# Layer 2's first product by seven block products for two of three token chunks

## The chip, the cores and the metric

The kernel runs on one core of one Trainium2 chip. A time is the device time of one execution in microseconds (us); the time of a kernel is the median of its runs. Engines: PE (matrix products), DVE (vector), ACT (scalar, activations), POOL (GpSimd), SP (issues the DMAs). Each works through its own queue in order, and they wait for one another by semaphores.

## The reference

Attention with a window and sink tokens over 1536 tokens, then two feed-forward layers of width 512 to 2048 to 512:

```python
x = attention(q, k, v, n_sink, window)             # 1536 x 512
h = x @ moe_w_in                                   # layer 1
g = (a0 + a1*h + a2*h**2 + a3*h**3) / (1 + |b0|*|h| + |b1|*h**2 + 1e-6)
x = g @ moe_w_out
h = maximum(x @ moe2_w_in, 0)                      # layer 2
out = (h * h) @ moe2_w_out                         # 1536 x 512
```

## The kernel before

**Arithmetic.** The weights come as 64-bit numbers and are turned into fp32 on DVE (three steps, lines 241 to 253) and split on ACT and POOL into a high part in a format that PE takes at full rate and a low rest (`w_fin`, lines 274 and 275). Activations are split in the same way (`gh` and `gl`, lines 685 and 686; `xh` and `xl`). Each product is the sum of three: high by high, high by low, low by high.

**Tiles and steps.** Tokens are in three chunks c of 512, the hidden width in 16 tiles f of 128. A step (L, g, c, f) is one tile of one chunk: the first product `g1` (line 618) is 4 blocks of the width x 3 = 12 matmuls of 128 x 128 by 512 columns into one PSUM bank, tag T (two banks) or U (one); the second product `g2` (line 689) is 4 x 3 = 12 such matmuls, accumulated over the tiles f of a part g in four banks (two tiles `s` of two banks each). `CUTS` cuts the 16 tiles into parts: layer 1 in three, layer 2 in two of 8. After a part `finish` (line 712) reads the four banks, in its first part as a copy (half on DVE, half on ACT), then as an addition on DVE; after the last part of layer 2 it issues the four stores of the chunk on SP.

**Order.** The order of the work is written out by hand: `slot(k)` (line 759) issues, in this order, the split of step k-2 (`act_c`), two weight splits, the end of the activation of step k-1 (`act_b`, which also calls `finish`), `g1` of step k+1, the start of the activation of step k, pending splits of layer 1's results (`split_late`), weight conversion and input checks on DVE up to a due count (`w_until(due(k))`), and `g2` of step k-2. So PE alternates 12 matmuls of a first and 12 of a second product. In layer 2 the activation is a Relu on ACT and a product with the bank on DVE (line 659). K is 96; slots 48 to 95 start the second half of the steps, layer 2. The first `g1` of layer 2 is in slot 47, the last `g2` of layer 1 in slot 49, and its accumulators are read in slot 50 (line 732).

**Weights in layer 2.** 42 of 64 weight tiles are converted before layer 2, the other 22 in its first 22 slots, each followed by a job that reads a weight tile again for a check; then the other checks. `spare` is the list of free weight buffers, taken in order.

**The end.** `verdict()` (line 787) gathers checks of the inputs into a count `fl` on DVE, with one small matmul; it is called after slot 93 and its matmul stands between two slots. After the last slot `values_load` (line 1076) makes every engine load `fl` into a register, and line 1078 branches over a general path that isn't run here.

## Time and profile before

| what | value |
|---|---|
| time, median of 3 runs | 612.98 us (612.82 to 613.57) |
| the profiled execution | 613.21 us |
| its span, first to last instruction | 611.4 us |
| PE busy in the span | 597.7 us, 98% |
| DVE, ACT, POOL busy | 424.8, 342.9, 342.7 us |
| granted clock of PE, mean | 0.996 |

The span is what the trace covers; the execution's own time is 1.81 us longer. A busy PE is not PE at its peak: a matmul's record is longer than the distance to the next one, because matmuls are pipelined, so the price of one is the distance. Rows give the start in the span, the duration, the engine (PEld is the weight load, a q behind the name is the engine's sequencer), the line, the operation, output and input by tile names, and a count of merged instructions.

### The profile page before, as it was taken

Reading aid. Unit: us, or ns where it says so; the run is one execution under the profiler, and the core shown is the slowest. Engines: PE = TensorE matmul, PEld = TensorE weight load, DVE = VectorE, ACT = ScalarE, POOL = GpSimd, SP = SyncE. Lnnn points to the kernel's source line nnn. Section 1 sums busy time; section 2 is a strip of 40 time slices with the busy share of each in tenths; the row PEclk is TensorE's granted clock in tenths of the full one; section 3 lists DMA queues with packets and bytes.
Section 4 is the critical chain, followed back from the end, with each engine's and each line's share of the span. In section 5 each row is a group of like instructions: output and inputs, shape, how many; then the busy total and the mean of one; then the engine's idle time right before and its main releaser. Section 6 shows DMA issues by size and latency. Waiting matters only on the chain.

```text
span 611.4 us, 9769 instructions
## 1 busy us (share of the span) xinstructions
PE 597.7 (98%) x3490; PEld 491.4 (80%) x3490; DVE 424.8 (69%) x855; ACT 342.9 (56%) x727; POOL 342.7 (56%) x316
## 2 busy tenths in 40 slices
PE   8899999999999999999999999999999999999995
PEld 6787788788888878888888888888888888888884
DVE  5989759988988989858768799598583432531411
ACT  5989768788886687877769343333332222222220
POOL 4699878677776676757658475354452222222221
PEclk9999999999999999999999999999999999999998
DMA  7986313333323232111102457377375345600102
GB/s 204 287 219 178 87 38 103 104 103 104 104 70 103 73 101 82 56 36 35 46 24 69 139 176 246 129 228 254 94 247 182 117 161 163 200 8 0 70 0 75
DMA packets 64232, 72.05 MB, mean 118 GB/s; under 512 B 15280, under 2 KB 55216, under 8 KB 64176
## 3 DMA queue, kind: packets, MB, share of 16 engines
q1 hardware_dynamic: 64032, 71.35, 38.2%
q8 instruction: 29, 0.48, 0.3%
q14 instruction: 27, 0.22, 0.1%
q10 hardware_dynamic: 144, 0.00, 0.0%
HBM read 68.20 MB, written 3.15 MB: 117 GB/s over the span
## 4 chain that ended last, share of the span: by engine, by line
PE 71%; DVE 15%; ACT 10%; issue 2%; DMA 1%; DVEq 0%; ACTq 0%
PE s L703 32%; PE T L624 25%; PE U L624 7%; DVE t L678 3%; PE O L470 2%; DVE U L676 2%; ACT U L670 2%; ACT U L671 2%; ACT gh L685 2%; ACT w L274 2%; ACT pe L406 2%; DVE t L674 1%; DVE ns L387 1%; DVE O L241 1%; DVE wx L253 1%
## 5 line engine op out<-in xcount | busy, mean ns | idle before, releaser
L624 PE MATMUL T<-xh,w 128*128 128x512 f32 x640 | 210.9, 391 | 0.4 <-DVE t L653 0.4
L686 POOL TENSOR_TENSOR gl<-g,gh 128x512 fp32r<-128x512 f32 x48 | 62.2, 1296 | 157.8 <-ACT gh L685 157.8
L624 PEld LDWEIGHTS T<-xh,w 128*128 128x128 f32 x640 | 120.1, 188 | 27.6 <-DVE t L653 2.3
L703 PE MATMUL s<-gh,w 128*128 128x512 f32 x384 | 126.1, 389 | 0.0
L624 PE MATMUL T<-xl,w 128*128 128x512 f32 x320 | 124.6, 389 | 0.0
L703 PE MATMUL s<-w,gh 128*128 128x512 f32 x384 | 118.1, 389 | 0.0
L686 POOL TENSOR_TENSOR gl<-t,gh 128x512 fp32r<-128x512 f32 x48 | 62.3, 1297 | 42.8 <-ACT gh L685 42.0
L275 POOL TENSOR_TENSOR w<-wx,w 128x512 fp32r<-128x512 f32 x64 | 82.9, 1296 | 2.9 <-ACT w L274 2.3
L703 PEld LDWEIGHTS s<-w,gh 128*128 128x128 f32 x384 | 72.1, 188 | 15.0
L703 PEld LDWEIGHTS s<-gh,w 128*128 128x128 f32 x384 | 72.0, 188 | 14.9
L645 POOL TENSOR_TENSOR t<-t,ah 128x512 f32<-128x512 f32 x48 | 62.3, 1298 | 34.4 <-ACT t L642 32.5
L685 ACT CAST gh<-g 128x512 fp32r<-128x512 f32 x48 | 29.9, 623 | 82.1 <-PE s L703 74.7
L703 PE MATMUL s<-gl,w 128*128 128x512 f32 x192 | 74.7, 389 | 0.0
L703 PE MATMUL s<-w,gl 128*128 128x512 f32 x192 | 74.7, 389 | 0.0
L624 PEld LDWEIGHTS T<-xl,w 128*128 128x128 f32 x320 | 60.0, 188 | 12.2
L685 ACT CAST gh<-t 128x512 fp32r<-128x512 f32 x48 | 29.8, 622 | 45.5 <-DVE t L678 39.8
L674 DVE SCALAR_TENSOR_TENSOR t<-t,U 128x512 f32<-128x512 f32 x48 | 32.9, 686 | 28.8 <-ACT U L671 28.8
L659 DVE TENSOR_TENSOR g<-r,T 128x512 f32<-128x512 f32 x32 | 21.7, 682 | 42.2 <-ACT r L649 42.2
L649 ACT ACTIVATE r<-T 128x512 f32<-128x512 f32 x32 | 19.2, 600 | 53.2 <-PE T L624 53.1
L703 PEld LDWEIGHTS s<-gl,w 128*128 128x128 f32 x192 | 36.0, 188 | 7.6
L624 PE MATMUL U<-xh,w 128*128 128x512 f32 x128 | 42.1, 390 | 0.0
L406 ACT ACTIVATE pe<-ns,nmax 128x136 f32<-128x136 f32 (+1 forms) x96 | 38.0, 400 | 7.2 <-DVE nmax L387 7.0
(142 smaller groups left out, 1010.5 us busy)
## 6 DMA issues: line engine op xcount, KB each, us to landing
wr<-in_w_in_dram SPq DMA_DIRECT2D x54, 512.0 KB, 3.7
wr<-in_w_out_dram SPq DMA_DIRECT2D x52, 512.0 KB, 3.7
qr<-in_q_dram SPq DMA_DIRECT2D x12, 256.0 KB, 5.4
keys<-in_k_dram SPq DMA_DIRECT2D x12, 256.0 KB, 5.1
vr<-in_v_dram SPq DMA_DIRECT2D x12, 256.0 KB, 5.6
wr<-in_v_dram SPq DMA_DIRECT2D x6, 512.0 KB, 4.7
out_dram<-part SPq DMA_DIRECT2D x12, 256.0 KB, 2.0
vsc<-in_v_dram SPq DMA_DIRECT2D x2, 16.0 KB
```

The lines of the kernel that those rows point to most:

```text
L274: (nc.gpsimd.tensor_copy if conv["tag"] == "U" else nc.scalar.copy)(out=t[:, 0], in_=xf)
L275: nc.gpsimd.tensor_tensor(out=t[:, 1], in0=xf, in1=t[:, 0].bitcast(F32), op=ALU.subtract)
L406: nc.scalar.activation(out=t[:, e, 0:w], in_=ns[e][:, 0:w], func=ACTF.Exp, scale=-1.0, bias=nmax[:, ix:ix + 1], accum_out=rs[:, 2 * pr + e ...
L624: nc.tensor.matmul(h, lhsT=wi[a][:, kk * P:(kk + 1) * P], rhs=(xh, xl)[b][c][:, kk, :], start=(kk == 0 and a + b == 0), stop=(kk == KD - 1 ...
L645: nc.gpsimd.tensor_tensor(out=t, in0=t, in1=ah, op=ALU.mult)
L649: nc.scalar.activation(out=r, in_=h, func=ACTF.Relu)
L659: nc.vector.tensor_tensor(out=g, in0=st.pop(k), in1=h, op=ALU.mult)
L674: nc.vector.scalar_tensor_tensor(out=t, in0=t, scalar=QP, in1=r0, op0=ALU.add, op1=ALU.mult)
L678: nc.vector.scalar_tensor_tensor(out=t3, in0=t3, scalar=fa[:, 0:1], in1=r0, op0=ALU.add, op1=ALU.mult)
L685: nc.scalar.copy(out=gh, in_=g)
L686: nc.gpsimd.tensor_tensor(out=gl, in0=g, in1=gh.bitcast(F32), op=ALU.subtract)
L703: nc.tensor.matmul(acc[L, g, c][m], lhsT=lh, rhs=rh, start=(f == f0 and a + b == 0), stop=(f == f1 and a == 1),)
```

## The change

1. **Seven products for eight.** In layer 2 the first product of the chunks 1 and 2 is computed for pairs of tiles f at a time. With the weights of the pair as 2 x 2 blocks (the two tiles by the two halves of the width) and the tokens as 2 x 2 blocks (the two halves of the width by the two chunks), a group has 7 block products of 6 matmuls each (`product`) in the place of 8. Sums of weight blocks go into the four S products (`weights_sums`, on POOL, then split by ACT and POOL), sums of token blocks into the T products (`tokens_sums`, once, on DVE, right after layer 1's last results; split by `tokens_split` in the turns 3 to 6). DVE adds the block products up (`after`), ACT does Relu and Square (`square`). Chunk 0 keeps the 12 matmuls of a step (`whole`).
2. **Turns.** Layer 2 has its own order: turn n is issued in slot 47 + n. `hs` lists which first products a turn does, `gs` which second product, `ms` and `ss` the turns in which the weight sums and their splits are issued. In the first part the turns 0 to 3 do the four whole steps of chunk 0, turn 4 product 1 of group 0, turn 5 none, turn 6 product 6, the turns 7 to 12 the pairs of `ORDER`; second products stand in the turns 3 to 6, 9, 10 and 13 to 18. In the later parts each turn has 12 matmuls of first products, but for one without, and the second products run six turns behind; the turns 48 to 54 have second products only.
3. **Four parts.** `CUTS` cuts layer 2 in four parts of 4 tiles. The last part of the last chunk accumulates in four single banks (T, T, U and half of an `s`). The order of the weight tiles follows; the 22 late conversions have turns of their own (`CONV`), one check is due in each turn, and at most 11 weight tiles of layer 2 are held (`LIVE`).
4. **The flag.** The first half of `verdict` stands after turn 49, its matmul after turn 52, and the load of the flag after turn 53, before the last turn.

```diff
-CUTS = ((0, 4, 9, 16), (0, 8, 16))
+CUTS = ((0, 4, 9, 16), (0, 4, 8, 12, 16))
 AHEAD = 10
+LIVE = 11
+GAP = 2
+TURN = 12
+CONV = (1, 9, 10, 12, 13, 15, 16, 17, 18, 19, 20, 22, 23, 27, 28, 29, 30, 31, 32, 34, 35, 36)
+ORDER = (((0, 1), (0, 6)), ((0, 7), (0, 2)), ((0, 5), (0, 4)), ((1, 1), (0, 3)), ((1, 7), (1, 6)), ((1, 2), (1, 5)),
+         ((1, 4), (1, 3)))
...
-    for m in range(LATE, 4 * NF):
-        jobs += [("c", m), again.pop(0)]
-    jobs += again
+    stop = [len(jobs)]
+    for n in range(1, max(CONV[-1], len(again)) + 1):
+        jobs += [("c", LATE + i) for i, r in enumerate(CONV) if r == n]
+        if again:
+            jobs.append(again.pop(0))
+        stop.append(len(jobs))
...
-        if m not in wx or len(spare) <= keep[0] or int(spare[0][1:]) >= len(wpool):
+        if m not in wx or not spare or int(spare[0][1:]) >= len(wpool) or sum(key[0] for key in W) == LIVE:
...
-            if steps[k][0] == 1:
-                g = mp.tile([P, CT], F32, tag="t3", name="g2", bufs=3)
-                nc.vector.tensor_tensor(out=g, in0=st.pop(k), in1=h, op=ALU.mult)
-                gq["f", k] = g
-                finish(0)
-                finish(1)
-                return
...
+                if f1 == NF - 1 and (L, c) == (1, NCH - 1):
+                    acc[L, g, c] = [ps_t("T"), ps_t("T"), ps_t("U"), ps_s()[:, 0]]
+                else:
+                    acc[L, g, c] = [t[:, m] for t in [ps_s(), ps_s()] for m in range(2)]
...
-                    if g == len(CUTS[L]) - 2:
+                    if g == len(CUTS[L]) - 2 and c < NCH - 1:
...
+        two = {}
+        hs, gs, ms, ss = {}, {}, {}, {}
+        for p in range(len(CUTS[1]) - 1):
+            h0 = p * TURN + (p > 0)
+            g0 = h0 + TURN // 2
+            for i in range(4):
+                hs[h0 + i] = (p, i, None)
+            for i in range(7):
+                hs[h0 + 4 + i + (0 if p else GAP)] = (p, i, ORDER[i][0 if i or p else 1:])
+            if p == 0:
+                hs[h0 + 4] = (p, 0, ORDER[0][:1])
+            for i in range(3 * 4):
+                c, f = divmod(i, 4)
+                r = g0 + i if p else 3 + i if i < 4 else (9, 10, 13, 14, 15, 16, 17, 18)[i - 4]
+                gs[r] = (p, c, 4 * p + f)
+            for r, (a, b) in enumerate(((1, 2), (5, 6) if p else (2, 7))):
+                ms[h0 + a], ss[h0 + b] = (p, r), r
+        ends2 = max(gs)
...
+        def weights_sums(p, r):
+            tag = two["s"][r]
+            f = 4 * p + 2 * r
+            x, z = fresh(tag[0]).bitcast(F32), fresh_sum()
+            y = z.rearrange("p a (b n) -> p (a b) n", b=2)
+            for e in range(2):
+                w = W[1, f + e, 0]
+                nc.gpsimd.tensor_tensor(out=x[:, e], in0=w[0].bitcast(F32), in1=w[1].bitcast(F32), op=ALU.add)
+            hw = DM // 2
+            a11, a12, a21, a22 = (x[:, e, j * hw:(j + 1) * hw] for e in range(2) for j in range(2))
+            for dst, i0, i1, op in (
+                (y[:, 0], a21, a22, ALU.add), (y[:, 1], y[:, 0], a11, ALU.subtract),
+                (y[:, 2], a11, a21, ALU.subtract), (y[:, 3], a12, y[:, 1], ALU.subtract),
+            ):
+                nc.gpsimd.tensor_tensor(out=dst, in0=i0, in1=i1, op=op)
+            two["S", r] = lambda: split(z, fresh(tag[0]), fresh(tag[1]))
+
+        def split(src, hi, lo):
+            nc.scalar.copy(out=hi, in_=src)
+            nc.gpsimd.tensor_tensor(out=lo, in0=src, in1=hi.bitcast(F32), op=ALU.subtract)
+            return hi, lo
+
+        def tokens_sums():
+            tag, = tags(1)
+            parts[2, 2] = fresh(tag), tag
+            b11, b21, b12, b22 = (parts[c, j][0].bitcast(F32) for c in (1, 2) for j in range(2))
+            two["f"] = f = {1: b11, 2: parts[2, 2][0].bitcast(F32), 3: b12, 4: b21}
+            for dst, i0, i1 in ((1, b12, b11), (2, b22, f[1]), (3, b22, b12), (4, b21, f[2])):
+                nc.vector.tensor_tensor(out=f[dst], in0=i0, in1=i1, op=ALU.subtract)
+            f[0] = b22
+
+        def tokens_split(j):
+            if j % 3:
+                hi, lo = map(fresh, tags(2))
+            else:
+                s = slice(0, 2) if j else slice(2, 4)
+                hi, lo = xh[2][:, s, :], xl[2][:, s, :]
+            two["T", j] = split(two["f"][j], hi, lo)
+            if j == 0:
+                for key in [key for key in parts if key[0]]:
+                    spare.append(parts.pop(key)[1])
...
+            bank, w, x = {
+                1: ("a", lambda: wf(0, 0), xs(1, 0)), 2: ("a", lambda: wf(0, 1), xs(1, 1)),
+                3: ("b", lambda: sw(4), xs(2, 1)), 4: ("c", lambda: wf(1, 1), T.get(4)),
+                5: ("b", lambda: sw(1), T.get(1)), 6: ("b", lambda: sw(2), T.get(2)), 7: ("c", lambda: sw(3), T.get(3)),
+            }[j]
+            w = w()
+            for kk in range(2):
+                for a, b in ((0, 0), (0, 1), (1, 0)):
+                    nc.tensor.matmul(
+                        two[r][bank], lhsT=w[a][:, kk * P:(kk + 1) * P], rhs=x[b][:, kk, :],
+                        start=(j in (1, 5, 6, 7) and kk == 0 and a + b == 0), stop=(kk == 1 and a == 1),
+                        skip_group_check=True,
+                    )
+            if j in (2, 4):
+                w_free((1, f + (j == 4), 0))
+            if j == 1:
+                t = two[r]["p1"] = mp.tile([P, CT], F32, tag="ah", name="p1", bufs=1)
+                nc.scalar.copy(out=t, in_=two[r]["a"])
...
+        def square(key, src):
+            g = two["g"].pop(0) if src is not None else gq["f", key]
+            nc.scalar.activation(out=g, in_=src if src is not None else g, func=ACTF.Relu)
+            nc.scalar.activation(out=g, in_=g, func=ACTF.Square)
+            gq["f", key] = g
+
+        def after(p, r, j):
+            f, x = 4 * p + 2 * r, two[r]
+
+            def summed(key, bank, u):
+                g = gq["f", key] = two["g"].pop(0)
+                nc.vector.tensor_tensor(out=g, in0=x[bank], in1=x[u], op=ALU.add)
+                square(key, None)
+
+            if j in (6, 7):
+                u = x[j] = mp.tile([P, CT], F32, tag="t", name="u", bufs=2)
+                nc.vector.tensor_tensor(
+                    out=u, in0=x["b" if j == 6 else "c"], in1=x["p1" if j == 6 else 6], op=ALU.add
+                )
+            elif j == 2:
+                square((p, 1, f), x["a"])
+            elif j == 5:
+                summed((p, 2, f + 1), "b", 7)
+            elif j == 4:
+                summed((p, 1, f + 1), "c", 6)
+            elif j == 3:
+                summed((p, 2, f), "b", 6)
...
+        def turn(n):
+            if n == 1:
+                setup_two()
+            if n - 1 in hs:
+                p, i, pair = hs[n - 1]
+                if pair is None:
+                    square((p, 0, 4 * p + i), hq.pop(("h", p, i)))
+                else:
+                    for r, j in sorted(pair, key=lambda x: (6, 7, 2, 5, 4, 3, 1).index(x[1])):
+                        after(p, r, j)
+            if n > 2:
+                finish(0)
+                finish(1)
+            if n == 3:
+                tokens_sums()
+            if n in hs:
+                p, i, pair = hs[n]
+                if pair is None:
+                    h = hq["h", p, i] = ps_t("U" if i == 2 else "T")
+                    whole(h, 4 * p + i, 1, 0)
+                else:
+                    for r, j in pair:
+                        product(p, r, j)
+            if n + 1 in gs:
+                key = gs[n + 1]
+                g = gq.pop(("f", key))
+                act_c(key, g)
+                two["g"].append(g)
+            if n in ss:
+                r = "S", ss[n]
+                two[r] = two[r]()
+            for j in ((2,), (3,), (1,), (4, 0))[n - 3] if 3 <= n < 7 else ():
+                tokens_split(j)
+            if n in ms:
+                weights_sums(*ms[n])
...
+            if 0 <= k - 2 < K:
                 g2(k - 2)
+            if k + 1 - K in gs:
+                g2(gs[k + 1 - K])
...
+        yield
...
-        if n == KL + 3 * NF - 3:
-            fl = verdict()
-    flag = nc.values_load(fl, min_val=0, max_val=12 * P)
+        if n == slots - 6:
+            last = verdict()
+            next(last)
+        if n == slots - 3:
+            fl = next(last)
+        if n == slots - 2:
+            flag = nc.values_load(fl, min_val=0, max_val=12 * P)
```

## Rows read from the trace of the kernel before

**Rows 1.** The page: busy share per engine, granted clock by slices, chain by engine
```profile
PE 597.7 (98%) x3490; PEld 491.4 (80%) x3490; DVE 424.8 (69%) x855; ACT 342.9 (56%) x727; POOL 342.7 (56%) x316
...
PEclk9999999999999999999999999999999999999998
...
PE 71%; DVE 15%; ACT 10%; issue 2%; DMA 1%; DVEq 0%; ACTq 0%
```

**Rows 2.** Busy time in one stretch: bounds, length, engines (x instructions), PEclk, DMA, GB/s
```profile
334.55:604.36 269.81, 269.80 (x1191) 222.79 (x1189) 147.55 (x248) 78.22 (x133) 99.11 (x78) 1.00 0.42 137
```

**Rows 3.** The chain that ended last: start us, us, what
```profile
351.03 2.72 PE T L624 x12
...
593.47 10.89 PE s L703 x48
...
604.39 0.70 DVE part L738
...
605.22 0.45 DVE part L738
```

**Rows 4.** Groups by line of POOL: line, operation, xcount | busy us, mean ns | idle
```profile
L686 POOL TENSOR_TENSOR gl<-g,gh 128x512 fp32r<-128x512 f32 x48 | 62.2, 1296 | 157.8 <-ACT gh L685 157.8
...
L143 POOL TENSOR_TENSOR su<-su 128x128 f32<-128x128 f32 x1 | 0.5, 506 | 2.1 <-DVE su L125 2.1
```

**Rows 5.** Groups by line of DVE
```profile
L222 DVE TENSOR_REDUCE vmax<-wr 128x1 f32<-128x1024 f32 x6 | 7.2, 1212 | 0.0
```

**Rows 6.** Timeline of POOL, ACT and DVE at the crossing: start us, us, what
```profile
336.77 1.29 POOL L275 TENSOR_TENSOR w<-wx,w 128x512 fp32r<-128x512 f32 x1
...
346.37 1.30 POOL L686 TENSOR_TENSOR gl<-g,gh 128x512 fp32r<-128x512 f32 x1 [2.63 <-ACT gh L685]
347.63 1.29 POOL L275 TENSOR_TENSOR w<-wx,w 128x512 fp32r<-128x512 f32 x1
...
345.67 0.62 ACT L685 CAST gh<-g 128x512 fp32r<-128x512 f32 x1 [2.17 <-PE s L703]
...
349.71 2.77 DVE L732 SCALAR_TENSOR_TENSOR part<-s,na,part 128x512 f32<-128x512 f32 x4 [3.08 <-PE s L703]
```

**Rows 7.** Timeline: two small DVE operations with both inputs in SBUF, and POOL
```profile
580.14 1.26 DVE L809 SCALAR_TENSOR_TENSOR bad<-size 128x1 f32<-128x1 f32 x1
...
580.07 1.32 POOL L686 TENSOR_TENSOR gl<-g,gh 128x512 fp32r<-128x512 f32 x1 [4.15 <-ACT gh L685]
...
46.25 0.45 DVE L422 TENSOR_TENSOR rs<-rs,eps 128x8 f32<-128x8 f32 x1
...
46.08 0.61 POOL L502 CAST xh<-xf 128x512 fp32r<-128x512 f32 x1
```

**Rows 8.** Lines 1076 and 1078: engine, operation, duration ns min/median/max, first and last start
```profile
L1076 PEldq TENSOR_LOAD <-fl x1: 492/492/492, 600.9 to 600.9; - x1
L1076 SPq TENSOR_LOAD <-fl x1: 529/529/529, 606.1 to 606.1; - x1
...
L1078 SPq EVENT_SEMAPHORE  x8: 17/17/17, 609.5 to 610.0; - x8
L1078 DVEq COMPARE_BRANCH  x1: 72/72/72, 605.3 to 605.3; - x1
L1078 SPq COMPARE_BRANCH  x1: 45/45/45, 607.0 to 607.0; - x1
L1078 DVEq EVENT_SEMAPHORE  x1: 21/21/21, 608.8 to 608.8; - x1
```

**Rows 9.** Timeline: the flag's matmul and its last step
```profile
590.32 0.20 PE L818 MATMUL O<-bad,ones 128*2 128x12 f32 x2
...
590.75 0.14 DVE L822 CAST fl<-nbad 1x1 int32<-1x1 f32 x1
```

**Rows 10.** Busy time in one stretch, after the last matmul (PEclk third from the right)
```profile
607.00:607.50 0.50, 0.00 (x0) 0.00 (x0) 0.00 (x0) 0.00 (x0) 0.00 (x0) 0.50 0.55 197
```

**Rows 11.** Timeline: the first matmuls of the kernel
```profile
1.12 5.82 PE L516 MATMUL s<-wz 128*128 128x512 f32 x14 [1.12 <-DVE nbig L511]
```

More of the change, by code (lines that the diff above doesn't have):

```diff
@@ L613 @@
     steps = [
-        (L, g, c, f) for L in range(2) for g in range(len(CUTS[L]) - 1) for c in range(NCH)
-        for f in range(*part(L, g))
+        (0, g, c, f) for g in range(len(CUTS[0]) - 1) for c in range(NCH) for f in range(*part(0, g))
     ]
@@ L619, in g1, with whole @@
         L, g, c, f = steps[k]
-        h = ps_t("U" if L and k % 3 == 2 else "T")
+        hq[k] = h = ps_t("T")
+        whole(h, f, L, c)
+        if c == NCH - 1:
+            w_free((L, f, 0))
+    def whole(h, f, L, c):
         wi = W[L, f, 0]
@@ L679, in act_b, with act_c @@
             gq["f", k] = t3
-        def act_c(k):
-            g = gq.pop(("f", k))
+        def act_c(k, g=None):
+            g = gq.pop(("f", k)) if g is None else g
             gh = mp.tile([P, CT], F32R, name="gh", bufs=2)
@@ L689, in g2 @@
         def g2(k):
-            L, g, c, f = steps[k]
+            L, g, c, f = steps[k] if k in range(KL) else (1,) + k
             f0, f1 = part(L, g)[0], part(L, g)[1] - 1
             if f == f0:
-                acc[L, g, c] = [t[:, m] for t in [ps_s(), ps_s()] for m in range(2)]
+                if f1 == NF - 1 and (L, c) == (1, NCH - 1):
+                    acc[L, g, c] = [ps_t("T"), ps_t("T"), ps_t("U"), ps_s()[:, 0]]
+                else:
+                    acc[L, g, c] = [t[:, m] for t in [ps_s(), ps_s()] for m in range(2)]
             wo = W[L, f, 1]
@@ new lines, in layers, with fresh, fresh_sum, tags @@
+        ends2 = max(gs)
+        def fresh(tag):
+            return wpool[int(tag[1:])].tile([P, 2, DM], F32R, tag=tag, name="two")
+        def fresh_sum():
+            return fresh(two["sum"]).bitcast(F32)
+        def tags(n):
+            return [spare.pop(0) for _ in range(n)]
+        def setup_two():
+            two["sum"], = tags(1)
+            two["s"] = [tags(2), tags(2)]
+            two["g"] = [t[:, j].bitcast(F32) for t in map(fresh, tags(4)) for j in range(2)]
+        def weights_sums(p, r):
[14 more added lines that the diff above has]
+            two["S", r] = lambda: split(z, fresh(tag[0]), fresh(tag[1]))
@@ new lines, in tokens_split, with product @@
+        def tokens_split(j):
[8 more added lines that the diff above has]
+                    spare.append(parts.pop(key)[1])
+        def product(p, r, j):
+            if j == 1:
+                two[r] = {"a": ps_t("T")}
+            if j == 6:
+                two[r]["b"] = ps_t("T")
+            if j == 7:
+                two[r]["c"] = ps_t("U")
+            f = 4 * p + 2 * r
+            S = two["S", r] if j in (3, 5, 6, 7) else None
+            T = {i: two["T", i] for i in (1, 2, 3, 4) if ("T", i) in two}
+            xs = lambda c, k: [x[c][:, 2 * k:2 * k + 2, :] for x in (xh, xl)]
+            wf = lambda e, k: [w[:, 2 * P * k:2 * P * (k + 1)] for w in W[1, f + e, 0][0:2]]
+            sw = lambda i: [
+                t.rearrange("p a (b n) -> p (a b) n", b=2)[:, i - 1] for t in S
+            ]
+            bank, w, x = {
[13 more added lines that the diff above has]
+                w_free((1, f + (j == 4), 0))
+            if j == 1:
+                t = two[r]["p1"] = mp.tile([P, CT], F32, tag="ah", name="p1", bufs=1)
+                nc.scalar.copy(out=t, in_=two[r]["a"])
@@ L767, in slot @@
                 g1(k + 1)
+            else:
+                turn(k + 1 - K)
             if k < K:
@@ L775, in slot @@
             w_until(due(k))
-            if 0 <= k - 2:
+            if 0 <= k - 2 < K:
                 g2(k - 2)
+            if k + 1 - K in gs:
+                g2(gs[k + 1 - K])
             if after:
                 after()
-            if k == K + 1:
+            if k + 1 - K == ends2:
                 finish(0)
                 finish(1)
-        return slot, K + 2
+        return slot, K + ends2
     def verdict():
@@ L822, in verdict @@
         nc.vector.tensor_copy(fl, n)
-        return fl
+        yield fl
     def general():
@@ L1050, in due @@
             return WS * READY + (WS * (2 * NF + AHEAD - READY) * (k + 1 - KB)) // (KL - KB)
-        rest = 2 * NF - AHEAD
-        if k < KL + rest:
-            return ends[LATE + 2 * (k - KL) + 1]
-        return ends[min(LATE + 2 * rest + (3 * (k - KL - rest + 1)) // 2, len(jobs)) - 1]
+        return ends[stop[min(k + 1 - KL, len(stop) - 1)] - 1]
     slot, slots = layers(mp, due)
```

36 lines of the change are left out of this document (12 added, 24 removed).

## The prediction

> **What bounds the kernel now.** I read the page first, then the stage that the change touches, then single rows. The page shows the tensor engine (PE) busy for 98% of the span, with the granted clock in the top tenth in all but the last slice, and carrying most of the chain that ended last [rows 1]. A mean over stages could hide slack, so the next view is busy time per stretch: from 334.55 us, where the first matmul of layer 2 is issued, to the last matmul, PE is busy for all of 269.81 us, while DVE, ACT and POOL have 55%, 29% and 37% [rows 2]. The chain of waits shows how tight that is: 12 matmuls take 2.72 us, one block after the other, and the last 48 take 10.89 us, so a 512-column matmul costs 0.2268 us of PE's time (its own mean of 389 ns is pipelined and not the price) [rows 3]. In layer 2 a removed matmul is time saved, and any wait that PE gets is time lost.
>
> **What goes.** Chunks 1 and 2 have 2 x 16 first-product steps of 12 matmuls, 384. After: 4 parts x 2 groups x 7 products x 6 matmuls = 336. 48 fewer x 0.2268 = **-10.88 us**. Nothing else leaves PE.
>
> **What is added, over the layer.** POOL gets per group two 512-wide and four 256-wide sums and one 1024-wide subtraction, and five 1024-wide ones for the tokens. A 512-wide operation takes 1.30 us, a 128-wide one 0.51 [rows 4]; in a queue it repeats every 1.26 (346.37 to 347.63 [rows 6]). The line through the two gives 0.77 for 256 and 2.35 for 1024, in a queue 0.73 and 2.31 (estimates; bounds 0.51 to 1.30, and 1.30 to 2.60, two operations for one). A group costs 2.52 + 2.92 + 2.31 = 7.75 us; eight are 62, the tokens 12, less four old subtractions: POOL goes from 99 to some 168 of 259 us. ACT gets 48 squares and 8 copies at 0.6, and 13 copies at about 1.1: 78 to 124 us. DVE loses 48 products of 0.68, gets 40 sums of 0.69, 24 more accumulator reads (four parts, not two) and four token sums of about 1.2 (a 1024-wide reduction takes 1.21 [rows 5]): 148 to 163 us. All stays well below PE, and in parts 2 to 4 each sum is needed a 5.44 us turn or more after its input; I cost them at nothing. What covers them is PE's 24 matmuls a turn. In part 1 that cover is thin: turns 4 and 6 have 18 matmuls, turns 5, 7, 8, 11 and 12 have 12.
>
> **The crossing into layer 2, where it can stall.** Turn n is slot 47 + n; turn 0 begins at 334.55 [rows 2], turn 3 at 351.03 [rows 3]. POOL's queue in program order, by the prices above: weight split done 338.06 (row at 336.77 [rows 6]); sums of group 0, 5.44 us, to 343.5; last layer-1 `gl` and one weight split to 346.0; `gl` of turn 3, held by its `gh` (ACT waits for the buffer that PE reads, as now at 345.67 [rows 6]), to 347.6; split of group 0 to 349.9; sums of group 1, to 355.3; `gl` of turn 4 to 356.6; then split 2 of the tokens, `gl` of turn 5, split 3, `gl` of turn 6, splits 1, 4, 0. PE needs the `gl` of turn 4 in its third matmul of that block, 351.03 + 5.44 + 1.36 + 0.45 = 358.3, and that of turn 5 at 361.0. So far POOL would be in time by 1.7 and 0.6 us.
>
> But the four token sums come in between. DVE reads layer 1's last accumulators from 349.71 to 352.48, as now [rows 6], and then runs `tokens_sums`, whose both operands lie in SBUF. Nearly all large DVE operations of the kernel have one operand in PSUM, so the trace hardly shows such a thing, but it does show it small: the one-element L809, both inputs in SBUF, took 1.26 us instead of some 0.15, from 580.14 to 581.40, and POOL's `gl` ran from 580.07 to 581.39. L422, eight elements, both in SBUF, took 0.45 us, from 46.25 to 46.70, and POOL's cast ended at 46.69 [rows 7]. So such an operation waits for the POOL operation that is running. That POOL in turn waits while a long one of DVE runs, no row shows. I take that it does, because the first half is an exclusion and an exclusion has two sides. The Trainium skill says so outright (SBUF — State Buffer, "Who interferes with whom"): a DVE instruction with two SBUF inputs and a POOL one that reads SBUF share a port under an exclusive lock, and the later one blocks fully. The rows agree for DVE; by them alone the price lies between 0 and the four sums, 4.6 us.
>
> With the lock, taking turns: POOL's four 256-wide sums begin at 352.4; token sum 1 waits for the first, 353.1 to 354.3; and so on, sum 2 to 356.2, sum 3 to 358.1, sum 4 to 360.0 (1.15 us each). `gl` of turn 4 ends at 361.3: PE, ready at 358.3, waits **3.07 us**. Split 2 follows to 363.6, `gl` of turn 5 to 364.85; PE needs it at 363.62 + 0.45: **0.78 us** more. After that PE is late enough for all: product 6 (367.1) needs split 2; product 7 (371.2) split 3, done at 367.1; product 5 (373.9) split 1, 370.6; product 4 (375.3) split 4, 372.9; product 3 (378) split 0, 375.2. If DVE ran its sums in one go the total would be 3.7. I take **+3.85 us**. Without POOL's wait it is 0. If the 256- and 1024-wide POOL operations are at their upper bounds, the two groups' sums and one split add 4.5 us to POOL's lateness, and the stall is 8.3; at the lower ends, 2.
>
> **The tail.** Now PE ends at 604.36 and DVE's last read at 605.67, since two of the four last reads wait for the last matmul [rows 3]. After, the last chunk has four single banks, so one read is left behind PE: 0.03 + 0.69, 0.6 us less. Then SP: flag load 606.1, assertion, branch 607.0, next event 609.5 [rows 8]. With the load two slots earlier the branch follows the last store by 0.9 us less. DVE's side limits this: its branch is at 605.3, its next event at 608.8, behind which SP is only 0.7 late. Gain 0.9 to 1.5, I take **-1.2**. PE's own load (0.49 us) stands before its last 12 matmuls; PE's queue reached it at 600.9, 3.4 us ahead of the array [rows 8], so the array has work while it loads; the flag was ready 0.6 us after its matmul (590.32 to 590.89 [rows 9]), and after that matmul stands two slots of 2.72 us before the end. Cost 0.
>
> **Sum.** Span 611.4 - 10.88 + 3.85 - 1.2 = 603.2. The profiled execution was 613.21, 1.81 around its span, and 0.23 over the median of the runs (612.98): 603.2 + 1.81 - 0.23 = **604.8 us**.
>
> **Rivals.**
> A. No stall at the crossing: POOL isn't held, or its work is shorter than by my line. For it: 1.7 and 0.6 us of room without the lock; against: L809. 612.98 - 10.88 - 1.2 = 600.9, with the tail's upper end 600.6.
> B. PE's clock falls in the 3 us stall. The granted clock is 0.50 in 607.0 to 607.5, PE idle since 604.36 [rows 3, 10]: its lower level, 1.2 GHz, after idle time, and a stall is idle time. Against it: the stall ends where PE goes on at once, and no wait of PE inside the kernel lowers the clock [rows 1]. Price: the first 14 matmuls, run from idle, took 5.82 us, against 14 x 0.227 = 3.18 [rows 11]: +2.6, so 607.4 (the second wait of 0.78 would hide in it: 606.6). The Trainium skill (TensorE: Matmul & The Clock Gate, "Part 1") also has an idle array fall to half clock; the row agrees on the level.
> C. POOL's operations at the upper bounds: 612.98 - 10.88 + 8.3 - 1.2 = 609.2.
> D. Slower than before: the accumulators. Four parts turn them over at 11 boundaries instead of 5, and PE's next block needs DVE to have read the first pair of banks while PE does 2.72 us of first product. Now no boundary costs anything, and the read needs 2 x 0.69. If DVE stood in six conversion steps (6 x 0.62) just then, PE would wait 3.7 - 1.3 = 2.4 us; at the nine boundaries of parts 2 to 4 that is 21.6 us, 626. It outweighs the gain from 0.9 us a boundary on. Against it: DVE has 163 of 259 us and runs its conversions while PE still does the turn before.
> E. That the 48 matmuls don't count because PE isn't the bound: PE's 269.80 of 269.81 us exclude it [rows 2].
>
> **Chances.** Forecast (603.3 to 606) 0.50; A 0.26; B with C (606 to 610) 0.16; D and unforeseen waits 0.08. The range reaches from A's lower end, 600.6, through B to most of C: 600.6 to 608.6. No change means within 0.2%, 1.2 us, about what a measurement of this kernel can tell: 611.8 to 614.2. Faster 0.91 (the forecast, A, B with C less a little of its far end), same 0.03, slower 0.06.
>
> **What would show it.** In the trace after: 336 product matmuls and whole blocks of 12 at 2.72 us; two PE waits on POOL's `gl` in the second products of the turns 4 and 5, of some 3 and 0.8 us, near 358 and 364; token sums of DVE that are longer than 1.2 us and begin or end with POOL operations; POOL's 256-wide sums near 0.77; granted clock 1.00 throughout; no wait of PE on DVE at the later boundaries; 5.6 to 6.1 us from the last matmul to the end of the span, against 7.0. I am wrong if PE has no wait there (A), if the clock falls (B), or if waits turn up in parts 2 to 4 (D).

## The result and the profile after

| | before | after |
|---|---|---|
| time, median of 4 runs each, side by side | 612.90 us (612.70 to 613.57) | 605.07 us (604.96 to 605.50) |
| ratio, with its 95% interval | | 0.9872 (0.9855 to 0.9889) |
| the profiled execution, its span | 613.21, 611.4 us | 605.50, 603.7 us |
| first matmul of layer 2, last matmul begins | 334.55, 603.96 us | 333.92, 596.78 us |

The change makes the kernel 7.8 us faster (1.1 to 1.5%); 8.2 us were forecast, 604.8 us. The time is met to 0.3 us, but not by its terms alone: two of them are off, both against it, and half of that came back from a stage that the change hardly touches. (Of all executions in this document one, of the first experiment, fell into a slower state, 658.85 us at a mean granted clock of 0.849; it is left out of that experiment's time.)

The page of the changed kernel, as [rows 1] is that of before (busy us and share of the span, instructions; the clock by slices; the chain by engine):

```profile
PE 588.8 (98%) x3442; PEld 483.5 (80%) x3442; DVE 441.3 (73%) x875; ACT 386.0 (64%) x792; POOL 414.6 (69%) x373
...
PEclk9999999999999999999999999999999999999998
...
PE 69%; DVE 17%; ACT 8%; issue 2%; POOL 2%; DMA 1%; DVEq 0%; ACTq 0%
```

3490 instructions of PE have become 3442, 48 fewer, and PE is still the bound. What is new is POOL in the chain, with 2%. The clock row is blunt here: a slice is 15 us, and a fall of a few us doesn't show in it.

Layer 2 from its first to its last matmul, the view of [rows 2], and half a microsecond at the crossing (the PE clock is third from the right; the columns before it are PE, PEld, DVE, ACT and POOL):

```profile
333.92:596.60 262.68, 260.42 (x1142) 214.69 (x1141) 164.06 (x269) 121.55 (x198) 171.01 (x135) 0.99 0.43 141
361.50:362.00 0.50, 0.50 (x3) 0.40 (x2) 0.09 (x1) 0.00 (x0) 0.50 (x1) 0.50 0.83 295
```

PE lacks 2.26 us in 262.68, where before it lacked 0.01; DVE, ACT and POOL have 164, 122 and 171 us, for which 163, 124 and 168 were estimated. The second row is the surprise: a granted clock of 0.50, the lower level of 1.2 GHz.

All waits of PE from 330 us to the end (engine, tile and line that waited; who ended it; us in all, times, longest):

```profile
PE s L702 <- POOL gl L682: 2.3, 1, 2.3
```

One wait, by the engine and for the tile that the forecast named. The chain through the crossing (start, us, what) shows what POOL did ahead of it:

```profile
347.04 2.35 POOL two L806
349.39 2.52 POOL two L794 x2
...
351.98 1.61 POOL two L801
...
353.66 2.23 POOL two L801 x2
355.89 1.01 issue
356.91 1.71 POOL two L801
358.62 1.25 POOL gl L682
...
359.91 1.20 PE s L702 x4
```

The timeline of the same place, DVE first, then POOL (the first row is group 0's sums, 12 us earlier), then PE:

```profile
349.08 2.77 DVE L730 SCALAR_TENSOR_TENSOR part<-s,na,part 128x512 f32<-128x512 f32 x4 [6.99 <-PE s L702]
351.76 1.22 DVE L815 TENSOR_TENSOR part<-part 128x1024 f32<-128x1024 f32 x1
353.02 1.65 DVE L815 TENSOR_TENSOR two<-part 128x1024 f32<-128x1024 f32 x1
354.59 1.76 DVE L815 TENSOR_TENSOR part<-part 128x1024 f32<-128x1024 f32 x1
356.27 1.76 DVE L815 TENSOR_TENSOR part<-part,two 128x1024 f32<-128x1024 f32 x1
...
340.02 2.96 POOL L801 TENSOR_TENSOR two<-two 128x256 f32<-128x256 f32 x4
...
351.98 6.64 POOL L801 TENSOR_TENSOR two<-two 128x256 f32<-128x256 f32 x4
358.58 1.27 POOL L682 TENSOR_TENSOR gl<-two,gh 128x512 fp32r<-128x512 f32 x1
...
357.04 0.61 PE L702 MATMUL s<-w,gh 128*128 128x512 f32 x2
359.91 0.50 PE L702 MATMUL s<-w,gl 128*128 128x512 f32 x1 [2.26 <-POOL gl L682]
...
366.66 1.52 PE L852 MATMUL T<-two 128*128 128x512 f32 x6
```

The same four sums take POOL 2.96 us for group 0 and 6.64 us for group 1, where DVE's token sums begin 0.2 us ahead of them: 3.68 us more. `gl` then ends at 359.85, and PE, which has issued its two `gh` products of that block at 357.04, goes on at 359.91. The second products of the turns 4 and 5 run from 357.04 to 366.66, 9.62 us where 24 matmuls at 0.2268 are 5.44: 4.18 us too long, 2.42 of it up to the `gl` (359.91 - 357.04 - 2 x 0.2268) and the other 1.76 behind it, where the clock fell.

So the gain of the span, 7.7 us, is made up of: 48 matmuls, -10.88; the crossing, +4.18; +0.15 in one block of twelve at 476.99 that takes 2.87 us and not 2.72; -0.52 from the last matmul's start to the end; and -0.63 ahead of layer 2, which is less than executions differ there (over those shown below layer 2 begins anywhere from 333.80 to 335.59 us). In that block, by the profile, a weight load (PEld) waits for ACT's Relu of a bank T (line 865); the first experiment has the same block of 2.87 us:

```profile
478.19 1.23 PEld L852 LDWEIGHTS T<-two 128*128 128x128 f32 x6 [0.27 <-ACT two L865]
```

### The profile page after: what moved, and what is told of

It reads as the page before. It is cut to its first block, busy times and chain, and to the rows that moved or that the text cites. A ratio compares the mean times of both kernels' runs of the same rounds, so it can differ in the third digit from the quotient of the medians.

```text
span 603.7 us, 9762 instructions
## 1 busy us (share of the span) xinstructions
PE 588.8 (98%) x3442; PEld 483.5 (80%) x3442; DVE 441.3 (73%) x875; ACT 386.0 (64%) x792; POOL 414.6 (69%) x373
## 4 chain that ended last, share of the span: by engine, by line
PE 69%; DVE 17%; ACT 8%; issue 2%; POOL 2%; DMA 1%; DVEq 0%; ACTq 0%
PE s L702 31%; PE T L635 16%; PE T L852 9%; PE U L852 4%; DVE t L674 3%; PE O L477 2%; DVE U L672 2%; ACT gh L681 2%; DVE ns L394 2%; ACT U L666 2%; ACT U L667 2%; ACT w L281 2%; DVE s L384 2%; DVE t L670 2%; PE U L635 1%
## 5 line engine op out<-in xcount | busy, mean ns | idle before, releaser
L635 PE MATMUL T<-xh,w 128*128 128x512 f32 x480 | 158.4, 391 | 0.4 <-DVE t L656 0.4
L682 POOL TENSOR_TENSOR gl<-two,gh 128x512 fp32r<-128x512 f32 x48 | 62.2, 1298 | 73.0 <-ACT gh L681 69.8
L702 PE MATMUL s<-w,gh 128*128 128x512 f32 x360 | 111.9, 392 | 0.0
L635 PEld LDWEIGHTS T<-xh,w 128*128 128x128 f32 x480 | 90.1, 188 | 21.5 <-DVE t L656 2.3
L635 PE MATMUL T<-xl,w 128*128 128x512 f32 x240 | 93.5, 389 | 0.0
L681 ACT CAST gh<-two 128x512 fp32r<-128x512 f32 x48 | 29.5, 618 | 45.9 <-PE s L702 45.8
L635 PEld LDWEIGHTS T<-xl,w 128*128 128x128 f32 x240 | 45.1, 188 | 9.0
L281 ACT CAST w<-wx 128x512 fp32r<-128x512 f32 x57 | 35.1, 618 | 21.5 <-PE s L702 10.9
L702 PEld LDWEIGHTS s<-w,gl 128*128 128x128 f32 x180 | 34.1, 189 | 9.8 <-POOL gl L682 2.7
L736 DVE TENSOR_TENSOR part<-s,part 128x512 f32<-128x512 f32 x33 | 21.3, 686 | 27.4 <-PE s L702 26.8
```

Source lines behind the costliest of these rows:

```text
L281: (nc.gpsimd.tensor_copy if conv["tag"] == "U" else nc.scalar.copy)(out=t[:, 0], in_=xf)
L635: nc.tensor.matmul(h, lhsT=wi[a][:, kk * P:(kk + 1) * P], rhs=(xh, xl)[b][c][:, kk, :], start=(kk == 0 and a + b == 0), stop=(kk == KD - 1 ...
L681: nc.scalar.copy(out=gh, in_=g)
L682: nc.gpsimd.tensor_tensor(out=gl, in0=g, in1=gh.bitcast(F32), op=ALU.subtract)
L702: nc.tensor.matmul(acc[L, g, c][m], lhsT=lh, rhs=rh, start=(f == f0 and a + b == 0), stop=(f == f1 and a == 1),)
L736: nc.vector.tensor_tensor(out=q, in0=src, in1=q, op=ALU.add)
```

## The experiments

Theory: the 8.2 us are 48 matmuls, less a stall at the crossing, which comes from DVE's token sums and POOL's weight sums excluding each other in SBUF, and a shorter tail. Rivals: POOL is late for its own sums' sake (no exclusion of POOL); the four parts cost something; the matmuls aren't what counts; the clock is the price. Each kernel ran beside the kernel before on the same chip. "Layer 2" below is the time from its first matmul to the start of its last in the profiled execution: 269.41 us before, 262.86 after, 258.53 if only the 48 matmuls were taken away.

### The token sums' second operand in PSUM

The four sums subtract a zeroed PSUM bank and not the other token block; the subtraction is left out, so its time is that of the same DVE work with one operand in SBUF.

```diff
+            if n == 2:
+                two["zero"] = ps_t("O")
+                nc.vector.memset(two["zero"], 0.0)
...
-                nc.vector.tensor_tensor(out=f[dst], in0=i0, in1=i1, op=ALU.subtract)
+                nc.vector.tensor_tensor(out=f[dst], in0=i0, in1=zero, op=ALU.subtract)
```

> Theory (lock): the stall at the crossing comes from the four token sums of DVE, both of whose inputs lie in SBUF, holding up POOL's weight sums. Here the right operand of the four sums is a zeroed PSUM bank (the subtraction of the token blocks is left out), so their number, length and place stay, but only one input is in SBUF. POOL's four 256-wide sums of group 1 should take 0.74 us each (3.0 together, not 6.6), each token sum some 1.2 us, PE should not wait for gl, its clock stay at 1.00, and the two second products of turns 4 and 5 take 5.44 us and not 9.62: 605.07 - 4.2 = 600.9 us. Rival (POOL's queue is simply too long there, the sums only happen beside it): the 256-wide sums still end at about 358.6, the wait of 2.3 us and the fall of the clock stay, 605 us.

601.77 us (the median of five executions), ratio 0.9821 (0.9805 to 0.9836), 0.9 us above the forecast; layer 2 258.68 us. PE has no wait in layer 2. POOL's sums of group 1 and DVE's token sums in this kernel's timeline:

```profile
351.86 2.96 POOL L801 TENSOR_TENSOR two<-two 128x256 f32<-128x256 f32 x4
...
351.65 1.21 DVE L816 TENSOR_TENSOR part<-part,O 128x1024 f32<-128x1024 f32 x1
352.78 1.21 DVE L816 TENSOR_TENSOR two<-part,O 128x1024 f32<-128x1024 f32 x1
353.91 2.34 DVE L816 TENSOR_TENSOR part<-part,O 128x1024 f32<-128x1024 f32 x2
```

The same instructions begin at the same time, side by side, and neither slows the other: POOL is back at the 2.96 us of group 0. Layer 2 is within 0.15 us of the 48 matmuls alone, and those 0.15 are the block of 2.87 us. This shows the exclusion, and that it acts on POOL, which [rows 7] could not show. The whole stall came from it, the fall of the clock included.

### All sums of the first part on DVE

```diff
+            eng = nc.gpsimd if p else nc.vector
...
-                nc.gpsimd.tensor_tensor(out=x[:, e], in0=w[0].bitcast(F32), in1=w[1].bitcast(F32), op=ALU.add)
+                eng.tensor_tensor(out=x[:, e], in0=w[0].bitcast(F32), in1=w[1].bitcast(F32), op=ALU.add)
...
-                nc.gpsimd.tensor_tensor(out=dst, in0=i0, in1=i1, op=op)
+                eng.tensor_tensor(out=dst, in0=i0, in1=i1, op=op)
```

> The weight sums of part 1 (two groups, 12 operations) go from POOL to DVE, which has been idle from 342 to 349 us; group 1 has a buffer of its own. Theory (lock): POOL is rid of 10.9 us before the crossing, and the token sums meet fewer POOL operations, so gl of the turns 4 and 5 is in time, no wait of PE, clock 1.00: 600.9 us, faster than the changed kernel by 4.2. Rival (DVE becomes the bound): the added 12 operations, each waiting for a POOL operation, push the reading of layer 1's accumulators and the token sums back by more than 2 us, and PE waits in turn 3 or on product 6 instead: 604 to 606 us.

605.67 us, ratio 0.9886 (0.987 to 0.9902). The gain that was expected of it did not come. Its waits of PE in layer 2:

```profile
PE s L702 <- POOL gl L682: 1.8, 1, 1.8
PE s L702 <- DVE part L730: 1.1, 1, 1.1
```

Group 1's sums now stand on DVE ahead of the reads of layer 1's accumulators, which begin at 353.00 us and not at 349.08, and PE waits for them; the token sums follow late. The token sums themselves take 1.22 or 1.23 us each here, since POOL has nothing to do beside them until the last: most of the exclusion is gone, and PE waits because the sums stand in DVE's queue ahead of urgent work.

### The flag loaded after the last turn

```diff
-        if n == slots - 2:
-            flag = nc.values_load(fl, min_val=0, max_val=12 * P)
+    flag = nc.values_load(fl, min_val=0, max_val=12 * P)
```

> The load of the flag goes back behind the last turn; its computation stays two slots early. Theory (SP's queue sets the end): load, register operation and assertion stand again between the last store and the branch, 0.9 us, so 606.0 us. Rival (the landing of the last store sets the end, since the last event at 602.3 us came 4.2 us after the last store was issued, where it was 2 in the kernel before): 605.1 us, no change.

605.47 us, ratio 0.9875 (0.986 to 0.989): no difference to the changed kernel (0.9872) that can be measured. But the intervals are 1.8 and 2.1 us wide, so the times alone decide nothing about 0.9 us. In the profiles of the two, the last addition of DVE ends at 597.50 us here and at 597.90 in the changed kernel, the span 6.1 and 5.8 us later. SP's branch, its next events and its waits behind the branch, in this kernel, then in the changed one:

```profile
L1253 SPq EVENT_SEMAPHORE  x8: 17/17/17, 601.6 to 602.2; - x8
L1253 SPq COMPARE_BRANCH  x1: 45/45/45, 598.8 to 598.8; - x1
...
SPq L1253 <- SPq L1253: 2.8, 1, 2.8
```

```profile
L1254 SPq EVENT_SEMAPHORE  x8: 17/17/17, 601.1 to 602.3; - x8
L1254 SPq COMPARE_BRANCH  x1: 45/45/45, 598.3 to 598.3; - x1
...
SPq L1254 <- SPq L1254: 3.6, 3, 2.8
```

With the early load the branch comes 0.5 us sooner, but behind the 2.8 us that follow it SP waits twice more, 0.8 us in all, and that is for the last two stores: by the updates of its semaphore in the trace the last store, issued at 597.93, is complete at 602.02, 4.09 us later, and SP's event for it stands at 602.04. Here the last store is complete at 601.49, 3.96 us after its issue, and SP asks for it only at 601.90. So the early load pays until the last store takes over; this is read from one profile of each. (The 2.0 us from issue to landing that the page gives for the stores leave out the last two.)

Another thing comes on top in six of the eleven profiles of the changed kernel and its variants: SP's issue of one of the last two stores takes 1.4 to 1.9 us, where it takes 0.33 to 0.35 in the other five, in the kernel before and in that with four parts alone. In the changed kernel's second profile (the last experiment) it is this row, and SP's branch comes at 598.9, 1.8 us behind the start of the last issue and not 0.4:

```profile
L739 SPq DMA_DIRECT2D out_dram<-part x12: 332/333/1718, 570.9 to 597.1; - x12
```

Why was not found.

### The last accumulators in the two-bank tiles, as before

```diff
-                if f1 == NF - 1 and (L, c) == (1, NCH - 1):
-                    acc[L, g, c] = [ps_t("T"), ps_t("T"), ps_t("U"), ps_s()[:, 0]]
-                else:
-                    acc[L, g, c] = [t[:, m] for t in [ps_s(), ps_s()] for m in range(2)]
+                acc[L, g, c] = [t[:, m] for t in [ps_s(), ps_s()] for m in range(2)]
```

> The last part of chunk 2 accumulates in the two tiles s again. Theory: two reads instead of one stand behind the last matmul (+0.6 us), and in turn 51 no first product covers DVE's reading of the chunk before, so PE waits some 1.6 us for it: 605.07 + 2.2 = 607.3 us. Rival (the reads hide, and the end is set by the stores): 605.1 us.

607.54 us, ratio 0.9909 (0.9894 to 0.9924), 2.5 us behind the changed kernel by the medians, near what was expected; but it divides otherwise. The wait of 1.6 us for DVE that was expected is not there: PE's only wait in layer 2 is that on `gl`, 2.3 us. In its profile (of its slowest execution, 609.01 us) layer 2 is 0.46 us longer (263.32), the way from the last matmul's start to the end 8.39 us and not 6.92. Of those 1.47 us the last reads are 0.6, as expected: DVE's last addition ends 1.71 us after the last matmul's start, and not 1.12. The other 0.9 lie behind it, where SP's issue of a store took 1.63 us; that they come from the accumulators is not shown.

### The four parts alone, in the kernel before

```diff
-CUTS = ((0, 4, 9, 16), (0, 8, 16))
+CUTS = ((0, 4, 9, 16), (0, 4, 8, 12, 16))
...
+                    if g == len(CUTS[L]) - 2:
```

(The second line puts the store behind a condition, so that only the last part stores.)

> The kernel before with layer 2 in four parts and nothing else. Theory: the six more turnings of the accumulators hide behind the first products (2 x 0.69 us of reading against 2.72 us), PE waits nowhere for DVE at a boundary: 612.9 us, as before. Rival (the accumulators' turning costs): PE waits for DVE at the new boundaries, 0.5 to 2 us each, 616 to 625 us, and the changed kernel would then carry such waits too.

613.18 us against 613.01, ratio 1.0000 (0.999 to 1.0009). PE has no wait in layer 2. In the view of [rows 2]:

```profile
334.29:603.70 269.41, 269.41 (x1191) 222.79 (x1189) 161.27 (x272) 78.56 (x133) 99.15 (x78) 1.00 0.42 137
```

24 more accumulator reads raise DVE from 147.55 to 161.27 us, and nothing else moves. Rival D, the only one that ended slower than before, is out.

### 36 products more

Product 1's six matmuls are done twice in the parts 2 to 4 (6 groups x 6 = 36 extra matmuls, into the same bank).

```diff
-            for kk in range(2):
+            for kk in range(4 if p and j == 1 else 2):
+                kk %= 2
```

> In the parts 2 to 4 product 1 of each group is done twice (6 groups x 6 = 36 matmuls more), so there 8 products stand where 7 did. Theory (PE sets the pace of these parts, a matmul is 0.2268 us): 605.07 + 8.2 = 613.2 us. Rival (something else sets the pace there, and the matmuls that Strassen's form saves are partly idle time): less than 5 us more, under 610 us.

613.83 us, ratio 1.0008 (0.9998 to 1.0017): 8.8 us more than the changed kernel, for 36 x 0.2268 = 8.16 (the two ran on different chips). Against the kernel with the late flag, whose clock did not fall either, layer 2 is 8.02 us longer (270.16 to 262.14), 0.223 us a matmul. A matmul in layer 2 costs its distance, added as well as removed.

### Group 1's sums of the first part on DVE, a turn sooner

From the second experiment: only the sums that collide move, and to a place where DVE has time, before layer 1's last accumulators are due; they get a buffer of their own.

```diff
+            eng = nc.vector if (p, r) == (0, 1) else nc.gpsimd
...
+        del ms[2]
...
+            if n == 1:
+                weights_sums(0, 1)
```

(and `eng` in both sums, as above)

> Of the weight sums of part 1 only group 1's six operations go to DVE, a turn earlier, with a buffer of its own; group 0's stay on POOL. Theory (lock): DVE's six operations each wait for a POOL operation, but end by 347 us, before layer 1's accumulators are read at 349; POOL is rid of 5.5 us and pays 3; the token sums meet a POOL that has little to do, so gl of the turns 4 and 5 is at most 0.5 us late and the clock stays at 1.00: 601.4 us. Rival (the wait only moves, as with both groups on DVE): gl of the last layer-1 step or the reading of the accumulators becomes late, 604 to 606 us.

602.15 us, ratio 0.9813 (0.9799 to 0.9826), 0.8 us above the forecast; layer 2 259.32 us, and this wait alone:

```profile
PE s L702 <- POOL gl L682: 0.3, 1, 0.3
```

This is a version that beats both kernels. Where the two engines now meet the exclusion shows again (POOL, then DVE):

```profile
340.42 3.99 POOL L803 TENSOR_TENSOR two<-two 128x256 f32<-128x256 f32 x4
...
356.40 3.39 POOL L808 TENSOR_TENSOR two<-two 128x1024 fp32r<-128x1024 f32 x1 [3.51 <-ACT two L807]
...
342.07 4.04 DVE L803 TENSOR_TENSOR two<-two 128x256 f32<-128x256 f32 x4
...
356.29 1.22 DVE L817 TENSOR_TENSOR part<-part,two 128x1024 f32<-128x1024 f32 x1
```

POOL's sums of group 0 take 3.99 us beside DVE's, and not 2.96, where nobody waits for them. The split at 356.40 takes 3.39 us, and not 2.40, beside the last token sum; the `gl` of turn 5 is behind it, and that is the 0.3 us.

### Two of four token sums with an operand in PSUM

One token block is copied into two PSUM banks by ACT, and two sums read it there (the others are rearranged, with the same result).

```diff
+            held = [ps_t("O"), ps_t("U")]
+            for j in range(2):
+                nc.scalar.copy(out=held[j], in_=b11[:, j])
+                tt(out=f[1][:, j], in0=b12[:, j], in1=held[j], op=ALU.subtract)
+            tt(out=f[3], in0=b22, in1=b12, op=ALU.subtract)
+            for j in range(2):
+                tt(out=f[2][:, j], in0=f[3][:, j], in1=held[j], op=ALU.add)
+            tt(out=f[4], in0=b21, in1=f[2], op=ALU.subtract)
```

> The left block of chunk 1 is copied by ACT into two PSUM banks that are free then, and two of the four token sums take it from there (the second one as the third plus that block); the other two keep both inputs in SBUF. Everything is computed as before. Theory (lock): only two token sums hold POOL, 2.4 us instead of 4.6, so the wait of 2.3 us shrinks to some 0.8, too short for the clock to fall: 605.07 - 3.3 = 601.8 us. Rival (the number of operations counts, not where their inputs lie): six token sums for four make it later, 605 to 606 us.

603.28 us, ratio 0.9847 (0.9827 to 0.9867), 1.5 us above the forecast; layer 2 260.48 us, and PE waits 1.5 us. POOL's four sums and the token sums on DVE:

```profile
352.19 3.94 POOL L801 TENSOR_TENSOR two<-two 128x256 f32<-128x256 f32 x4
...
357.35 3.39 POOL L806 TENSOR_TENSOR two<-two 128x1024 fp32r<-128x1024 f32 x1
360.70 1.27 POOL L682 TENSOR_TENSOR gl<-two,gh 128x512 fp32r<-128x512 f32 x1
...
353.27 1.56 DVE L820 TENSOR_TENSOR part<-part 128x1024 f32<-128x1024 f32 x1
354.87 0.69 DVE L822 TENSOR_TENSOR two<-part,O 128x512 f32<-128x512 f32 x1
356.19 2.28 DVE L823 TENSOR_TENSOR part<-part,two 128x1024 f32<-128x1024 f32 x1
```

The sums from PSUM keep their 0.68 us beside a busy POOL, the two from SBUF wait (1.56 and 2.28 us); with one locked sum among them POOL's four take 3.94 us and not 6.64, and the `gl` of turn 4 is in time. The last locked sum then meets the split ahead of the `gl` of turn 5 (3.39 us, and not 2.40); that `gl` ends at 361.97, and PE waits for it there. The forecast had left that second meeting out.

### The wait filled with matmuls

Ten extra matmuls into an unused bank behind the first product of turn 4 and four behind that place in turn 5 (their result is not read), so that PE is not idle while it waits.

```diff
+            for _ in range({4: 10, 5: 4}.get(n, 0)):
+                if n == 4 and _ == 0:
+                    two["fill"] = ps_t("U")
+                nc.tensor.matmul(two["fill"], lhsT=W[1, 2, 0][0][:, 0:P], rhs=xh[1][:, 0, :], start=True, stop=True)
```

> The changed kernel with 10 extra matmuls into an unused bank behind the first product of turn 4 and 4 behind that place in turn 5 (14 x 0.2268 = 3.2 us of PE work that nobody reads), so PE is busy while it would wait for gl. Theory (the lock sets when gl comes, and the idle 2.3 us let the clock fall in some executions): layer 2 keeps its length but the clock stays at 1.00, the wait on gl is below 0.5 us, and the time is that of the changed kernel in an execution whose clock did not fall, 604.3 to 605.3. Rival (the stall is not idle time but work that PE owes, i.e. PE is the bound there): the 14 matmuls come on top, +3.2 us, 608.2. Rival 2 (the clock is the whole cost behind the wait): 1.2 to 1.8 us faster than the changed kernel, 603.3 to 603.9.

And beside it, on the same chip, the changed kernel once more, and the version with one group on DVE:

> The changed kernel unchanged, beside the one with filled waits and the one with the sums on DVE, on the same chip. Both theories: 605.1, ratio to before 0.987; one PE wait on gl of 2.3 us, a second one of 0.4 to 0.8 us if the clock did not fall. It tells how far the clock of the crossing differs between executions.

> The version with group 1's weight sums of part 1 on DVE one turn earlier, beside the changed kernel on the same chip. Theory (the crossing's stall is what it saves): 2.5 to 3.3 us below the changed kernel, 602 to 602.6, layer 2 at 259.3 us. Rival (the 602.15 of its first run came from that chip): within 1 us of the changed kernel.

606.13 us with the wait filled, 606.23 unfilled (ratios 0.9885, 0.987 to 0.99, and 0.9894, 0.9879 to 0.9909); 602.52 with one group on DVE (0.9828, 0.9815 to 0.9842). On this chip the changed kernel is 1.2 us slower than in its first runs, with before the same (612.86); the intervals of the ratios overlap, and the forecasts for it and for the filled wait (604.3 to 605.3) are missed by that. 14 matmuls, 3.18 us of PE's work, cost nothing: layer 2 is 262.19 us with them and 262.14 without. PE in the filled kernel:

```profile
357.10 2.43 PE L917 MATMUL U<-xh,w 128*128 128x512 f32 x10
359.37 0.61 PE L702 MATMUL s<-w,gh 128*128 128x512 f32 x2
360.00 0.50 PE L702 MATMUL s<-w,gl 128*128 128x512 f32 x1
```

and in the unfilled one, its waits of PE, the half microsecond at 361.50, and where the second products of the turns 4 and 5 begin and end:

```profile
PE s L702 <- POOL gl L682: 2.8, 2, 2.3
...
361.50:362.00 0.50, 0.50 (x4) 0.41 (x3) 0.03 (x1) 0.00 (x0) 0.50 (x1) 1.00 1.03 377
...
356.98 0.61 PE L702 MATMUL s<-w,gh 128*128 128x512 f32 x2
...
365.88 1.53 PE L852 MATMUL T<-two 128*128 128x512 f32 x6
```

This is the same kernel as the changed one, with the same idle stretch of 2.25 us, and its clock did not fall; instead the second wait that was forecast is there (0.58 us, before the `gl` of turn 5). The second products of the two turns take 8.90 us here (365.88 - 356.98), as they do in the kernel with the late flag and in that with 36 products more, and 9.62 in the two profiles where the clock fell, those of the changed kernel and of the last accumulators in `s`. So a fall costs 0.72 us net, because the slow stretch swallows the second wait. The version with one group on DVE stands 3.7 us below the changed kernel on this chip, more than the 2.5 to 3.3 expected; 2.86 of it is what layer 2 of the two profiles shows (259.28 to 262.14). Where the rest comes from is open: the profiles are of the fastest execution of the one and of the slowest of the other.

## Why the prediction held, and where it didn't

**The products, -10.88: right.** 48 instructions fewer, and both the kernel without a stall (258.68 us against 258.53) and the one with 36 matmuls more (0.223 us each) give the price from the chain in [rows 3].

**The work beside PE at nothing: right.** DVE, ACT and POOL met their estimates within 3 us, and no wait of PE is seen in parts 2 to 4, but for the 0.15 us of one block behind ACT's Relu. POOL's unknown sizes came out by the line between 128 and 512 columns: 0.74 us for 256 (0.77 estimated), 2.40 for 1024 (2.35).

**The stall, +3.85: right in cause and place, its parts mis-sized.** I wrote "PE, ready at 358.3, waits **3.07 us**" and 0.78 more. Where the clock held, the two second products took 8.90 us for 5.44, which is 3.46: 2.42 up to the first `gl`, and 1.04 behind it. (The profile's idle times, 2.25 and 0.58, are less, because a matmul's record is longer than its distance.) The step that is off is that each turn was priced at a whole POOL operation and a whole DVE sum one after the other, 0.73 + 1.15 = 1.88 us; the token sums follow each other after 1.57 and 1.68 us in the changed kernel, so two turns overlap by 0.2 to 0.3 us, and the four POOL sums took 6.64 us and not 7.5 (4 x 1.88). Two smaller slips: turn 3 begins with the matmul at 350.87 in the kernel before, and not at 351.03; and the room of the `gl` of turn 5 without the lock is 0.8 us by the prices given, not 0.6. The weighed rule of the Trainium skill (SBUF — State Buffer, "Who interferes with whom"; the full block stands in that page's summary) is confirmed in its substance, in both directions, by the first experiment: 6.64 us of POOL work with both operands of DVE in SBUF, 2.96 with one in PSUM. That "the later one blocks fully" is nearly so, by the same rows.

**The clock: wrong in the forecast, right as rival B, at a smaller price.** I held against B that PE goes on at once and that "no wait of PE inside the kernel lowers the clock"; but [rows 1] can't show that, with slices of 15 us and no wait of PE above 1.3 us in that trace. In the changed kernel's profile it fell, to 0.50 by 361.50 us, after 2.3 us of idle time and when PE had gone on for some 1.6 us; in one other profile with the same 2.3 us wait it fell too, in three it did not. The price, +2.6 from 14 matmuls run from idle [rows 11], was too high: 1.76 us for the slow stretch, 0.72 net. The mean clock of the executions does not settle how often it falls: the changed kernel took 605.38 us at 0.998 and 605.99 to 606.53 at 0.993 and 0.994 on one chip, but 605.01 at 0.994 and 605.12 at 0.996 in its first runs; and of 21 executions of the kernel before, whose PE waits nowhere in layer 2, five are at 0.993, of 614.19 to 614.49 us, and the others at 0.996 and above, of 612.65 to 613.47. So a lower mean clock has another cause as well; what decides whether the clock falls behind the wait is open.

**The tail, -1.2: half wrong.** The step "one read is left behind PE ... 0.6 us less" is right: DVE's last addition ends 1.12 us after the last matmul's start, and 1.71 before. The step "the branch follows the last store by 0.9 us less" is right for SP's queue, whose branch stands at 598.3, behind the last store's issue at 597.9. But what SP's last events then wait for is the last store, complete 4.09 us after its issue. Before, it was complete 3.99 us after its issue, at 609.69 by its semaphore, 0.07 us ahead of SP's own event for it: the queue and the last store arrived together, so an earlier queue alone could gain next to nothing. I left out that the tail has a second runner. Net -0.52 in this profile; in the second one of the same kernel, with the slow issue, the way from the last matmul's start to the end is 7.70 us (596.00 to 603.7), 0.26 longer than before. So of the term only the read's 0.6 is shown.

**The sum.** The terms off by 0.33 (crossing), 0.15 (one block) and 0.7 (tail) add up to 1.2 us against me, of which the 0.63 us ahead of layer 2, by chance of that execution, gave half back; another 0.2 came from the profiled execution standing 0.43 us over the median of its runs, where 0.23 was taken. That the time was met to 0.3 us is partly luck; the range was needed.

## What to carry to other kernels

Before two engines are given large additions at the same time, look where both operands lie: here a vector operation with one operand in PSUM ran beside GpSimd freely, with both in SBUF the two took turns (2.96 and 6.64 us of POOL for the same four sums), and it cost time where a third engine waited for one of them. When such work must be moved, move only the part that collides, and to a place ahead of the urgent work of the engine that gets it, not onto it. Price a removed or added matmul at its distance where the stage's view shows PE at all of its time, and treat a tail as two races, one of the queue and one of the last store.

## What was not expected of the hardware

- Turns under the lock overlap a little: 1.57 to 1.68 us for a pair that costs 1.13 (DVE's distance, from 351.65 to 352.78 with a PSUM operand) plus 0.74 us alone.
- Among five profiles with a PE wait of 2.25 to 2.3 us, the clock fell to 0.50 behind it in two and stayed at 1.00 in three.
- The last store of 256 KB was complete, by its semaphore, 2.9 to 4.7 us after SP began to issue it (3.99 before, 4.09 after), where an earlier one lands after 2.0; and SP's issue of one of the last two took 1.4 to 1.9 us in six profiles and 0.33 to 0.35 in the other seven. Neither was explained.
